# A polysketch attention with a rational feed-forward layer: buffers and linear parts by group instead of by chunk, with a new order

## The chip, the cores and the metric

The kernel runs on one core of a Trainium2 chip. The time is the device time of one execution in microseconds, the median of three runs. The profile is of one such execution. Engines: PE is TensorE (PEld its weight loads), DVE is VectorE, ACT is ScalarE, POOL is GpSimd, SP is SyncE. SP and ACT issue the plain loads and stores, POOL the accumulating transfers.

## What is computed

Attention with a feature map of 64 products for each head, for 4 batches, 4 heads, 1088 tokens and 32 dimensions, gives x of 4352 x 128. A feed-forward layer with 2048 hidden units follows; its activation is a rational function.

```python
def phi(x):
    a = np.einsum('rd,bhsd->bhsr', S1, x)          # r = 8
    b = np.einsum('rd,bhsd->bhsr', S2, x)
    return np.einsum('bhsi,bhsj->bhsij', a, b).reshape(*x.shape[:-1], r * r)
q_p, k_p = (phi(q), phi(k))
kv = np.einsum('bhsf,bhsd->bhfd', k_p, v)
z = np.sum(k_p, axis=2)
num = np.einsum('bhsf,bhfd->bhsd', q_p, kv)
den = np.einsum('bhsf,bhf->bhs', q_p, z)[..., None] + 1e-06
# x = num / den, heads put side by side
h = x @ w_in                                        # 128 -> 2048
h2 = h * h
P = a[0] + a[1] * h + a[2] * h2 + a[3] * h2 * h
Q = 1.0 + np.abs(b[0]) * np.abs(h) + np.abs(b[1]) * h2
return (P / (Q + 1e-06)) @ w_out
```

## The kernel before

The tokens are worked on in chunks of 512 (eight of them, 0 to 7) and a last one of 256 (8). For each chunk, h is computed transposed, 128 hidden units at a time: 16 slices of 128 x 512. The slices are taken in groups of 8 (g4 and g5 are chunk 1, ... g16 and g17 chunk 7); the first chunk has groups of 2, 2, 4 and 8 (g0 to g3), the last of 8, 4 and 4 narrower slices (g18 to g20). A full group is thus a tile of 128 x 4096 bf16, 1 MB.

The parameters are scaled so that Q is a constant times (1 + |y| + y^2) plus an offset, and 1/Q comes from a logarithm and an exponential on ACT. These are the steps of a group (names as in the text):

```python
h_mm       # PE:  h_ps = w_in^T x, two slices in a PSUM tile of 1024 (three tiles)
h_evac  e  # ACT (or DVE): hb = h_ps, to bf16
d_sq       # DVE: s = hb * hb                  tensor_tensor
d_ab       # DVE: u = |hb|                     tensor_scalar (bit mask)
us         # u += s                            accumulating DMA from POOL, or DVE
d_hi       # DVE: t = a3 * hb + a2             tensor_scalar
d_cu       # DVE: t = t * s                    tensor_tensor
d_lo       # DVE: hb = a1 * hb + a0            tensor_scalar
ts         # t += hb                           accumulating DMA from POOL, or DVE
ln, ex     # ACT: u = exp(-ln(... u + 1))
d_ov       # DVE: t = t * u                    tensor_tensor
project pj # PE:  out_ps += t^T w_out
```

Which sums and copies go to DVE is a table (ENGINE), and the order in which all steps are issued is a list of numbers (ORDER) found by a search. Each engine works through its own steps in that order. Buffers are taken when a step is issued and come free when the last step that gives them has been issued. In the kernel before, the buffers of the feed-forward part hold a whole chunk:

```python
BUFS = dict(xT=3, hb=2, s=1, u=2, t=2, ..., h_ps=3, out_ps=1, w_ps=1, ...)
FW = NF * CW                                        # 16 * 512 = 8192
SHAPES = dict(..., hb=([128, FW], BF), s=([128, FW], BF), u=([128, FW], BF), t=([128, FW], BF), ...)

WIDE = ["hi", "lo"]
def units(op):
    return whole if op in WIDE and 0 < n < len(chunks) else parts
...
def add(name, dst, src, f0, f1):
    if ENGINE.get(name) == "DVE":
        nc.vector.tensor_add(out=at(dst, f0, f1), in0=at(dst, f0, f1), in1=at(src, f0, f1))
    else:
        nc.gpsimd.dma_start(out=at(dst, f0, f1), in_=at(src, f0, f1), accum_op=AX.add, max_dma_last_dim=4096)
...
wide("sq", d_sq, "s", tt, ["e"])
wide("ab", d_ab, "u", ts, ["e"])
sum_of("us", "u", "s", ["sq", "ab"], [("s", n)])
wide("hi", d_hi, "t", tp, ["e", c_inv])
wide("cu", d_cu, None, tt, ["hi", "sq"], give=[("s", n)])
wide("lo", d_lo, None, tp, ["hi", "ab", "sq"])
sum_of("ts", "t", "hb", ["cu", "lo"], [("hb", n)])
```

So in chunks 1 to 7 the two linear parts, hi and lo, are one instruction each for the whole chunk (128 x 8192), and all else goes by group. Both kernels cut the first chunk's x into two halves of its tokens (SPLIT), so that the first h starts on the first half.

Before and beside this, for each batch the keys' features are made (transposes on PE, an evacuation, a projection, an evacuation `ea` of its first part, a product `pd` on DVE), kv is accumulated on PE and spread by four small copies (`s0`, `s1`, two each), and for each chunk of queries there are an evacuation `ev`, two expansions on PE, an evacuation `A`, a product on DVE, num and den on PE, a division of three DVE instructions, and a transpose with an evacuation `xe` that scales x by a number from the parameter b. An evacuation `eT` brings the output from PSUM. "Fills" are matmuls of zeros, two each, that only keep PE's clock up.

Of the kernel before, what the change touches and what calls it, by code (L numbers as in the profile page):

```python
# [12 lines left out]
FP = mybir.dt.float32  # L13
# [9 lines left out]

WIDE = ["hi", "lo"]
SPLIT = [0]
FILLS = 16

BUFS = dict(xT=3, hb=2, s=1, u=2, t=2, k_sb=2, v=1, q=2, L=1, h_ps=3, out_ps=1, w_ps=1,
# [3 lines left out]
    "ld.S0": "ACT", "ld.S1": "ACT", "ld.a": "ACT", "ld.b": "ACT", "k00.ea": "DVE", "k01.ea": "DVE", "k0.s0": "DVE",  # L32
    "q1.xe": "DVE", "k10.ea": "DVE", "k11.ea": "DVE", "k1.s0": "DVE", "k1.s1": "DVE", "q3.ev": "DVE", "k2.s1": "DVE",
    "k3.s0": "DVE", "q6.xe": "DVE", "q7.xe": "DVE", "g2.us": "DVE", "g4.e2": "DVE", "g4.us": "DVE", "g6.ts": "DVE",
    "g13.e0": "DVE", "g15.ts": "DVE", "g16.ts": "DVE", "g20.us": "DVE", "g19.ts": "DVE", "o8.eT": "DVE",
}

SKIP = ["f5", "f2", "f4", "f10", "f1"]

HOME = {  # L40
    "sT": "h_ps", "k01.T": "h_ps", "k01.ab": "h_ps", "kr.T": "h_ps", "kr.ab": "h_ps", "q0.T": "h_ps",
    "q0.xT.0": "h_ps", "q1.T": "h_ps", "q1.xT": "h_ps", "k10.T": "h_ps", "k11.T": "h_ps", "k11.ab": "h_ps",
    "kv.1": "h_ps", "q2.T": "h_ps", "q2.xT": "h_ps", "q3.T": "h_ps", "q3.xT": "h_ps", "k21.T": "h_ps",
    "kv.2": "h_ps", "q5.T": "h_ps", "k31.T": "h_ps", "q6.T": "h_ps", "q6.xT": "h_ps", "q7.xT": "h_ps",
    "fill.1": "h_ps", "fill.2": "h_ps", "fill.4": "h_ps", "fill.5": "h_ps", "fill.8": "h_ps", "fill.9": "h_ps",
    "fill.11": "h_ps", "fill.12": "h_ps", "fill.13": "h_ps", "fill.15": "h_ps",
# [3 lines left out]
    6, 28, 26, 30, 27, 1, 56, 0, 31, 32, 57, 4, 41, 42, 36, 7, 70, 71, 43, 37, 33, 58, 8, 20, 5, 38, 44, 46, 45, 60,  # L50
    59, 47, 21, 48, 81, 82, 49, 39, 40, 29, 51, 50, 52, 61, 53, 2, 72, 54, 3, 34, 55, 62, 74, 22, 10, 83, 64, 86, 87,
    23, 84, 85, 65, 66, 63, 67, 96, 97, 9, 73, 75, 68, 88, 89, 90, 218, 69, 219, 35, 220, 247, 11, 239, 235, 251, 16,
    221, 76, 222, 223, 255, 236, 224, 225, 77, 226, 12, 240, 248, 256, 252, 78, 24, 249, 227, 228, 243, 241, 229,
    237, 259, 25, 263, 231, 233, 245, 230, 244, 264, 232, 257, 234, 79, 253, 261, 98, 267, 271, 275, 80, 281, 100,
    242, 238, 260, 282, 268, 283, 265, 266, 250, 285, 287, 284, 286, 288, 254, 289, 290, 291, 292, 107, 246, 269,
    270, 273, 272, 258, 276, 91, 299, 262, 108, 99, 92, 93, 297, 101, 13, 95, 94, 301, 293, 102, 103, 104, 274, 118,
    295, 294, 105, 119, 296, 300, 298, 106, 309, 303, 109, 277, 278, 14, 133, 319, 321, 134, 111, 123, 320, 306, 304,
    279, 120, 18, 322, 124, 15, 110, 112, 305, 302, 310, 323, 324, 280, 325, 121, 307, 326, 122, 335, 327, 144, 328,
    145, 311, 113, 114, 115, 337, 313, 329, 125, 331, 333, 330, 135, 126, 127, 332, 334, 116, 137, 308, 160, 161,
    315, 117, 357, 339, 359, 312, 341, 338, 336, 361, 358, 128, 314, 360, 362, 347, 316, 129, 344, 342, 340, 130,  # L60
    131, 132, 343, 348, 136, 138, 363, 364, 162, 163, 365, 17, 139, 366, 140, 345, 141, 367, 164, 349, 19, 346, 368,
    369, 142, 143, 375, 373, 377, 370, 317, 371, 372, 318, 351, 395, 155, 146, 374, 376, 378, 379, 353, 396, 156,
    350, 397, 398, 399, 148, 400, 157, 170, 147, 171, 401, 382, 380, 383, 149, 385, 403, 405, 402, 150, 151, 158,
    381, 352, 384, 404, 406, 152, 159, 411, 413, 409, 386, 389, 407, 408, 172, 174, 153, 154, 410, 354, 355, 356,
    165, 387, 417, 414, 412, 433, 391, 434, 415, 166, 167, 168, 388, 435, 436, 420, 169, 437, 438, 418, 173, 175,
    416, 423, 390, 439, 440, 441, 181, 442, 419, 424, 443, 392, 449, 445, 176, 177, 421, 444, 182, 183, 422, 178,
    446, 451, 192, 179, 180, 427, 453, 425, 447, 448, 455, 393, 394, 473, 452, 450, 429, 185, 426, 471, 472, 454,
    474, 475, 476, 456, 184, 186, 477, 193, 458, 461, 187, 188, 459, 189, 479, 478, 480, 428, 194, 196, 462, 190,
    195, 191, 197, 457, 487, 489, 481, 482, 483, 460, 484, 485, 486, 430, 465, 488, 198, 199, 490, 463, 491, 431,
    432, 492, 464, 493, 511, 466, 496, 494, 509, 467, 510, 497, 513, 512, 514, 515, 516, 527, 495, 499, 200, 468,  # L70
    517, 518, 519, 521, 500, 520, 201, 523, 547, 522, 524, 549, 525, 529, 469, 470, 501, 498, 526, 503, 531, 502,
    528, 537, 211, 504, 532, 505, 205, 548, 534, 553, 550, 530, 506, 507, 215, 533, 551, 538, 558, 213, 564, 535,
    555, 508, 552, 208, 541, 539, 554, 560, 217, 557, 566, 536, 556, 563, 561, 559, 562, 570, 567, 573, 540, 543,
    210, 542, 214, 572, 569, 216, 580, 581, 565, 576, 577, 578, 544, 571, 575, 202, 545, 546, 568, 574, 209, 579,
    582, 583, 584, 585, 586, 587, 588, 207, 204, 589, 206, 212, 203,
# [40 lines left out]
def kernel(  # L116
# [27 lines left out]
    FW = NF * CW  # L144
# [14 lines left out]
    SHAPES = dict(xT=([128, CW], FP), hb=([128, FW], BF), s=([128, FW], BF), u=([128, FW], BF), t=([128, FW], BF),  # L159
# [408 lines left out]
    def add_chunk(n, W, sizes, g0, x_step, prev_o, store):  # L568
        rem = n == len(chunks)
        nsub = 1024 // W  # L570
        parts, f0 = [], 0
        for z in sizes:
            parts.append((f"g{g0 + len(parts)}", f0, f0 + z))
            f0 += z
        whole = [(f"w{n}", 0, NF)]

        def units(op):
            return whole if op in WIDE and 0 < n < len(chunks) else parts

        def at(buf, f0, f1):  # L580
            return T[buf, n][:, f0 * W:f1 * W]

        def h_mm(f0, cols=None):
            p = new("h_ps", n, f0) if cols in (None, 0) else T["h_ps", n, f0]
            c0, c1 = (0, W) if cols is None else (cols * W // 2, (cols + 1) * W // 2)
            for i in range(nsub):
                fi = f0 + i
                nc.tensor.matmul(p[:, i * W + c0:i * W + c1], lhsT=w_in_sb[:, fi * 128:(fi + 1) * 128],  # L588
                                 rhs=T["xT", n][:, c0:c1], start=True, stop=True)

        def h_evac(name, f0):
            if f0 == 0:
                new("hb", n)
            copy(name, at("hb", f0, f0 + nsub), T["h_ps", n, f0])

        def d_sq(f0, f1):
            nc.vector.tensor_mul(out=at("s", f0, f1), in0=at("hb", f0, f1), in1=at("hb", f0, f1))  # L597

        def d_ab(f0, f1):
            nc.vector.tensor_scalar(out=at("u", f0, f1).bitcast(mybir.dt.int16), in0=at("hb", f0, f1).bitcast(mybir.dt.int16),  # L600
                                    scalar1=0x7FFF, scalar2=None, op0=AX.bitwise_and)

        def d_hi(f0, f1):
            nc.vector.tensor_scalar(out=at("t", f0, f1), in0=at("hb", f0, f1), scalar1=a_sb[:, 3:4], scalar2=a_sb[:, 2:3],  # L604
                                    op0=AX.mult, op1=AX.add)

        def d_cu(f0, f1):
            nc.vector.tensor_mul(out=at("t", f0, f1), in0=at("t", f0, f1), in1=at("s", f0, f1))  # L608

        def d_lo(f0, f1):  # L610
            nc.vector.tensor_scalar(out=at("hb", f0, f1), in0=at("hb", f0, f1), scalar1=a_sb[:, 1:2], scalar2=a_sb[:, 0:1],  # L611
                                    op0=AX.mult, op1=AX.add)

        def add(name, dst, src, f0, f1):
            if ENGINE.get(name) == "DVE":
                nc.vector.tensor_add(out=at(dst, f0, f1), in0=at(dst, f0, f1), in1=at(src, f0, f1))  # L616
            else:
                nc.gpsimd.dma_start(out=at(dst, f0, f1), in_=at(src, f0, f1), accum_op=AX.add, max_dma_last_dim=4096)  # L618

        def ln(f0, f1):  # L620
            nc.scalar.activation(out=new("L", n, f0)[:, :(f1 - f0) * W], in_=at("u", f0, f1), func=ACT.Ln, bias=one_ap, scale=lsc)  # L621

        def ex(f0, f1):
            nc.scalar.activation(out=at("u", f0, f1), in_=T["L", n, f0][:, :(f1 - f0) * W], func=ACT.Exp, scale=-1.0)  # L624

        def d_ov(f0, f1):
            nc.vector.tensor_mul(out=at("t", f0, f1), in0=at("t", f0, f1), in1=at("u", f0, f1))  # L627
# [157 lines left out]
```

## Time and profile before

| | |
|---|---|
| time | 250.15 us, median of 3 runs (250.06 to 250.33) |
| span of the profiled execution | 248.3 us, mean granted TensorE clock 0.978 |
| accumulating transfers u<-s of 1 MB | 14, median 9.5 us from issue to landing |
| accumulating transfers t<-hb of 1 MB | 12, median 8.7 us |
| DVE, first polynomial instruction of g0 | at 25.77 us |
| DVE, last instruction (output evacuation) | at 244.60 us |
| DVE waiting for t<-hb; ACT waiting for u<-s | 1.0 us; 2.9 us in all |

How the profile is read. A line of the busy list gives each engine's busy time and its share of the span. A row of digits gives the busy share in 40 equal slices, in tenths. A queue line gives packets, MB, and the time that its packets took as a share of the 16 DMA engines. A line of the table by windows begins with the window and its length; then come the busy us of PE, PEld, DVE, ACT and POOL with the instruction counts, the granted clock, the DMA share and GB/s. A line of the chain gives the start, the duration and the work. A group line has the source line, engine, operation, tiles and shapes, count, then busy us and mean ns of one, and at the end the idle time ahead of it and its cause.

### The profile page before, as it was taken

The page shows a single profiled execution, that of the slowest core. Times are in us where ns is not written, and L with a number is a line of the kernel's source. Part 1 is how long each engine was busy: PE and PEld are TensorE (multiplying, and loading weights), DVE is VectorE, ACT ScalarE, POOL GpSimd, SP SyncE. Part 2 cuts the span into 40 slices and gives each one's busy share as a digit, 9 for nine tenths or more (in the row PEclk, how much of TensorE's full clock was granted, in tenths as well). Part 3 has the DMA queues.
Part 4 walks back from the last instruction along what each step waited for, and adds up shares of the span by engine and source line. Part 5 has one row for each costly group of instructions (what it writes and reads, how often), then busy time and mean ns, then how long its engine had stood idle before and what let it go on. Part 6 is the DMA issues. An engine that isn't in the chain of part 4 may idle for free.

```text
span 248.3 us, 4269 instructions
## 1 busy us (share of the span) xinstructions
PE 223.7 (90%) x1785; PEld 130.3 (53%) x1785; DVE 229.1 (92%) x204; ACT 215.5 (87%) x161; POOL 49.3 (20%) x59
## 2 busy tenths in 40 slices
PE   8979999999999999999999999998999966780773
PEld 4656444475745547546456735553465525650652
DVE  1658999999999899999999999999999999999993
ACT  3532579989999999999999999998999799999990
POOL 4000514210222110103231050202133021103120
PEclk9999999999999999999999999999999999997679
DMA  6796394979289999769999969999999989396872
GB/s 206 203 298 208 53 128 86 185 139 221 82 161 203 190 170 164 187 117 197 162 172 191 209 108 183 188 209 179 174 160 198 202 145 182 86 201 117 163 144 65
DMA packets 22627, 41.18 MB, mean 166 GB/s; under 512 B 5200, under 2 KB 13520, under 8 KB 22608
## 3 DMA queue, kind: packets, MB, share of 16 engines
q0 software_dynamic: 10432, 30.94, 71.7%
q1 hardware_dynamic: 11712, 9.90, 12.5%
q8 instruction: 14, 0.23, 0.4%
q10 hardware_dynamic: 464, 0.08, 0.2%
q14 instruction: 5, 0.04, 0.1%
HBM read 8.79 MB, written 2.23 MB: 44 GB/s over the span
## 4 chain that ended last, share of the span: by engine, by line
PE 60%; DVE 20%; DMA 9%; issue 5%; ACT 4%; POOLq 0%; DVEq 0%; ACTq 0%
PE h_ps L588 34%; PE out_ps L634 7%; PE h_ps L483 6%; DVE t L627 5%; DMA u<-s 5%; PE h_ps L503 3%; DVE t L608 3%; DVE t L604 2%; PE h_ps L405 2%; DVE hb L611 2%; DVE s L597 2%; DMA t<-hb 2%; DMA b_sb<-in_moe_b_dram 2%; DVE u L600 2%; ACT hb L187 2%
## 5 line engine op out<-in xcount | busy, mean ns | idle before, releaser
L588 PE MATMUL h_ps<-xT,w_in_sb 128*128 128x512 f32 (+1 forms) x292 | 125.2, 572 | 2.6 <-ACT xT L537 2.1
L588 PEld LDWEIGHTS h_ps<-xT,w_in_sb 128*128 128x128 f32 x292 | 52.7, 190 | 55.8 <-issue 43.5
L187 ACT CAST hb<-h_ps 128x1024 bf16<-128x1024 f32 x66 | 65.9, 1019 | 9.9 <-PE h_ps L588 9.4
L621 ACT ACTIVATE L<-u,one_ap,lsc 128x4096 f32<-128x4096 bf16 (+2 forms) x21 | 66.4, 3163 | 3.0 <-DMA u<-s 2.9
L624 ACT ACTIVATE u<-L 128x4096 bf16<-128x4096 f32 (+2 forms) x21 | 62.5, 2976 | 0.2
L634 PE MATMUL out_ps<-w_out,t 128*128 128x128 bf16 x544 | 36.9, 230 | 13.6 <-DVE t L627 13.6
L618 POOL DMA_DIRECT2D u<-s x18 | 25.9, 1436 | 116.0 <-DVE s L597 61.5
L634 PEld LDWEIGHTS <-t 128*128 128x128 bf16 x544 | 34.1, 104 | 21.9 <-DVE t L627 18.6
L627 DVE TENSOR_TENSOR t<-t,u 128x4096 bf16<-128x4096 bf16 (+2 forms) x21 | 39.3, 1880 | 1.4 <-DMA t<-hb 1.0
L597 DVE TENSOR_TENSOR s<-hb 128x4096 bf16<-128x4096 bf16 (+2 forms) x21 | 39.5, 1879 | 0.6 <-ACT hb L187 0.5
L608 DVE TENSOR_TENSOR t<-t,s 128x4096 bf16<-128x4096 bf16 (+2 forms) x21 | 39.4, 1878 | 0.1
L618 POOL DMA_DIRECT2D t<-hb x17 | 20.0, 1260 | 73.5 <-DVE t L608 52.6
L611 DVE TENSOR_SCALAR hb<-hb,a_sb 128x8192 bf16<-128x8192 bf16 (+3 forms) x14 | 23.2, 1657 | 0.1
L604 DVE TENSOR_SCALAR t<-hb,a_sb 128x8192 bf16<-128x8192 bf16 (+3 forms) x14 | 22.0, 1569 | 0.3 <-ACT hb L187 0.3
L600 DVE TENSOR_SCALAR u<-hb 128x4096 int16<-128x4096 int16 (+2 forms) x21 | 21.3, 1017 | 0.0
L483 PE MATMUL h_ps<-qT,Srep 64*128 64x512 f32 (+1 forms) x72 | 19.5, 617 | 0.4 <-DVE x L517 0.3
L503 PEld LDWEIGHTS h_ps<-kv,q_pT 128*64 128x64 f32 (+1 forms) x288 | 8.9, 134 | 7.2 <-issue 5.6
L490 DVE TENSOR_TENSOR q_pT<-A_sb,h_ps 128x1024 f32<-128x1024 f32 (+1 forms) x9 | 10.4, 1157 | 0.8 <-PE h_ps L483 0.7
L503 PE MATMUL h_ps<-kv,q_pT 128*64 128x66 f32 (+1 forms) x288 | 10.4, 225 | 0.6 <-DVE q_pT L490 0.6
L187 ACT COPY A_sb<-h_ps 128x1024 f32<-128x1024 f32 (+1 forms) x9 | 8.8, 973 | 0.6 <-PE h_ps L483 0.4
L483 PEld LDWEIGHTS h_ps<-qT,Srep 64*128 64x128 f32 x72 | 5.4, 184 | 5.9 <-ACT hb L187 2.6
L616 DVE TENSOR_TENSOR t<-t,hb 128x4096 bf16<-128x4096 bf16 (+1 forms) x4 | 7.5, 1886 | 0.0
(89 smaller groups left out, 139.6 us busy)
## 6 DMA issues: line engine op xcount, KB each, us to landing
u<-s POOLq DMA_DIRECT2D x14, 1024.0 KB, 9.5
t<-hb POOLq DMA_DIRECT2D x12, 1024.0 KB, 8.7
q<-in_q_dram SPq DMA_DIRECT2D x8, 256.0 KB, 4.8
k_sb<-in_k_dram SPq DMA_DIRECT2D x4, 512.0 KB, 5.7
v<-in_v_dram SPq DMA_DIRECT2D x4, 512.0 KB, 6.8
out_dram<-oT SPq DMA_DIRECT2D x8, 256.0 KB, 6.2
w_in_sb<-in_moe_w_in_dram SPq DMA_DIRECT2D x2, 512.0 KB, 5.6
t<-hb POOLq DMA_DIRECT2D x2, 512.0 KB, 5.6
```

What stands on the lines that cost most here:

```text
L187: nc.scalar.copy(out=out, in_=in_)
L483: nc.tensor.matmul(pair(i)[:, g, :W], lhsT=Srep[i][rows].rearrange("p g f -> p (g f)"), rhs=T["qT", n][rows, :W], start=True, stop=True)
L588: nc.tensor.matmul(p[:, i * W + c0:i * W + c1], lhsT=w_in_sb[:, fi * 128:(fi + 1) * 128], rhs=T["xT", n][:, c0:c1], start=True, stop=True)
L597: nc.vector.tensor_mul(out=at("s", f0, f1), in0=at("hb", f0, f1), in1=at("hb", f0, f1))
L604: nc.vector.tensor_scalar(out=at("t", f0, f1), in0=at("hb", f0, f1), scalar1=a_sb[:, 3:4], scalar2=a_sb[:, 2:3], op0=AX.mult, op1=AX.add)
L608: nc.vector.tensor_mul(out=at("t", f0, f1), in0=at("t", f0, f1), in1=at("s", f0, f1))
L611: nc.vector.tensor_scalar(out=at("hb", f0, f1), in0=at("hb", f0, f1), scalar1=a_sb[:, 1:2], scalar2=a_sb[:, 0:1], op0=AX.mult, op1=AX.add)
L618: nc.gpsimd.dma_start(out=at(dst, f0, f1), in_=at(src, f0, f1), accum_op=AX.add, max_dma_last_dim=4096)
L621: nc.scalar.activation(out=new("L", n, f0)[:, :(f1 - f0) * W], in_=at("u", f0, f1), func=ACT.Ln, bias=one_ap, scale=lsc)
L624: nc.scalar.activation(out=at("u", f0, f1), in_=T["L", n, f0][:, :(f1 - f0) * W], func=ACT.Exp, scale=-1.0)
L627: nc.vector.tensor_mul(out=at("t", f0, f1), in0=at("t", f0, f1), in1=at("u", f0, f1))
L634: nc.tensor.matmul(T["out_ps", n][:, j * 128:(j + 1) * 128], lhsT=T["t", n][:, fi * W + j * 128:fi * W + (j + 1) * 128], rhs=W_out[:, fi, ...
```

## The change

The feed-forward steps are written by group again. Every one of them, hi and lo too, works on its group's 128 x 4096; the four kinds of buffers are half as wide and twice as many, so that they take the same room, and a group takes and gives back its own. The engines of some sums and copies, the places of small PSUM tiles, the fills, the loads' order and the order of all steps come from another search, which allowed for ACT and DVE instructions to overlap. What it is for: each buffer comes free with its group instead of with its chunk, which gives the order more freedom; the price is twice as many instructions for hi and lo.

```diff
-WIDE = ["hi", "lo"]
-BUFS = dict(xT=3, hb=2, s=1, u=2, t=2, k_sb=2, v=1, q=2, L=1, h_ps=3, out_ps=1, w_ps=1,
+BUFS = dict(xT=3, hb=4, s=2, u=4, t=4, k_sb=2, v=1, q=2, L=1, h_ps=3, out_ps=1, w_ps=1,
 ENGINE = {
     "ld.S0": "ACT", "ld.S1": "ACT", "ld.a": "ACT", "ld.b": "ACT", "k00.ea": "DVE", "k01.ea": "DVE",
-    "k0.s0": "DVE", "q1.xe": "DVE", "k10.ea": "DVE", "k11.ea": "DVE", "k1.s0": "DVE", "k1.s1": "DVE",
-    "q3.ev": "DVE", "k2.s1": "DVE", "k3.s0": "DVE", "q6.xe": "DVE", "q7.xe": "DVE",
-    "g2.us": "DVE", "g4.e2": "DVE", "g4.us": "DVE", "g6.ts": "DVE", "g13.e0": "DVE", "g15.ts": "DVE",
-    "g16.ts": "DVE", "g20.us": "DVE", "g19.ts": "DVE", "o8.eT": "DVE",
+    "kr.ea": "DVE", "k0.s0": "DVE", "q1.ev": "DVE", "q1.xe": "DVE", "k10.ea": "DVE", "q3.xe": "DVE",
+    "k20.ea": "DVE", "k30.ea": "DVE", "k31.ev": "DVE", "q6.xe": "DVE", "q8.ev": "DVE", "q8.A": "DVE",
+    "q8.xe": "DVE", "g1.us": "DVE", "g1.ts": "DVE", "g6.e6": "DVE", "g17.us": "DVE", "o7.eT": "DVE",
+    "g18.us": "DVE", "g20.us": "DVE", "g20.ts": "DVE", "o8.eT": "DVE",
 }
-SKIP = ["f5", "f2", "f4", "f10", "f1"]             # fills left out
+SKIP = ["f2", "f10", "f8"]
 ...                                                # HOME and ORDER: other lists
-    FW = NF * CW
+    GW = GF * CW                                   # 8 * 512 = 4096
-    SHAPES = dict(..., hb=([128, FW], BF), s=([128, FW], BF), u=([128, FW], BF), t=([128, FW], BF), ...)
+    SHAPES = dict(..., hb=([128, GW], BF), s=([128, GW], BF), u=([128, GW], BF), t=([128, GW], BF), ...)
 ...
-        wide("hi", d_hi, "t", tp, ["e", c_inv])
-        wide("cu", d_cu, None, tt, ["hi", "sq"], give=[("s", n)])
-        wide("lo", d_lo, None, tp, ["hi", "ab", "sq"])
-        sum_of("ts", "t", "hb", ["cu", "lo"], [("hb", n)])
+        d2 = plan.add(nm + ".ab", "DVE", ts, d_abs, after=[he], take=[("u", g)])
+        d1 = plan.add(nm + ".sq", "DVE", tt, d_sq, after=[he], take=[("s", g)])
+        us = add_sum(nm + ".us", "u", "s", [d1, d2], [("s", g)])
+        hi = plan.add(nm + ".hi", "DVE", tp, d_high, after=[he, c_inv], take=[("t", g)])
+        p = plan.add(nm + ".cu", "DVE", tt, d_cube, after=[hi, d1], give=[("s", g)])
+        w = plan.add(nm + ".lo", "DVE", tp, d_low, after=[hi, d2, d1])
+        tsum = add_sum(nm + ".ts", "t", "hb", [p, w], [("hb", g)])
 ...
```

In the new order the first loads are q of chunk 1, k of batch 0, q of chunk 0 and the second half of w_in, then k's rest, k of batch 1 and v of batch 0; the parameter b is issued from ACT two copies earlier. Of the fills, one pair comes at g11 and two at g12 and g13, the others near the end; before, all were near the end.

## The prediction

> **What bounds the kernel now.** I read the page first: the busy line, the DMA row of the forty slices, the DMA queues.
>
> ```profile
> PE 223.7 (90%) x1785; PEld 130.3 (53%) x1785; DVE 229.1 (92%) x204; ACT 215.5 (87%) x161; POOL 49.3 (20%) x59
> ...
> DMA  6796394979289999769999969999999989396872
> ...
> q0 software_dynamic: 10432, 30.94, 71.7%
> q1 hardware_dynamic: 11712, 9.90, 12.5%
> ```
>
> Three engines are within 14 us of one another, and the 16 DMA engines carry 71.7 + 12.5 = 84% of the span. No single engine is "the" bound, so the second view is the table by windows (busy us of each engine in 25 us, then the granted clock, the DMA share and GB/s):
>
> ```profile
> 50.00:75.00 25.00, 25.00 (x244) 15.04 (x243) 24.74 (x21) 23.74 (x18) 4.71 (x3) 1.00 0.75 152
> 75.00:100.00 25.00, 25.00 (x243) 15.00 (x242) 23.90 (x18) 23.24 (x21) 3.57 (x3) 1.00 0.99 177
> 100.00:125.00 25.00, 25.00 (x156) 12.70 (x155) 24.86 (x17) 24.69 (x19) 5.91 (x4) 1.00 0.84 168
> 125.00:150.00 25.00, 25.00 (x225) 14.42 (x224) 24.89 (x18) 24.55 (x19) 6.28 (x4) 1.00 0.93 171
> 150.00:175.00 25.00, 24.01 (x182) 12.90 (x180) 24.71 (x20) 24.16 (x17) 4.76 (x4) 1.00 1.02 188
> 175.00:200.00 25.00, 24.26 (x176) 13.59 (x174) 24.90 (x18) 23.23 (x16) 5.81 (x4) 1.00 0.98 180
> 200.00:225.00 25.00, 16.80 (x115) 11.44 (x113) 24.49 (x14) 24.93 (x15) 3.47 (x4) 1.00 0.77 148
> ```
>
> From 50 to 200 us PE, DVE and ACT all have under 8% of idle time, and from 75 us on the DMA share is 0.84 to 1.02. The reader should see that everything is full at once: work taken from one engine is only worth something if it isn't put on another that has no room. The third view, the chain that ended last, changes owner accordingly: TensorE from 19 to 155 us, DVE and ACT with some accumulating DMAs after that.
>
> ```profile
> 145.72 3.63 PE h_ps L588 x8
> ...
> 183.45 11.74 DMA u<-s
> ...
> 235.78 5.14 DMA t<-hb
> ```
>
> The transfer issued at 183.45 took 11.74 us because another megabyte, issued at 179.98 us by the GpSimd timeline, was ahead of it: a queue, not a latency. The same view limited to 125 to 200 us, for the queues, gives the price of one:
>
> ```profile
> q0 software_dynamic: 3279, 12.60, 94.3%
> q1 hardware_dynamic: 432, 0.79, 3.1%
> ```
>
> 12.60 MB are 12 transfers of 1 MB, and 94.3% of 75 us is 70.7 us: 5.9 us of all 16 engines for each.
>
> **The Trainium skill.** "VectorE: DVE Perf Modes", section "The perf-mode tier table", puts bf16 tensor_scalar at four elements per cycle and tensor_tensor at two, and the section on the TRN2 errata says that each instruction pays a fixed part that a larger tile pays once. The trace agrees:
>
> ```profile
> L597 DVE TENSOR_TENSOR s<-hb 128x4096 bf16<-128x4096 bf16 x15 | 34.3, 2287 | 0.6 <-ACT hb L187 0.5
> L604 DVE TENSOR_SCALAR t<-hb,a_sb 128x8192 bf16<-128x8192 bf16 x7 | 16.9, 2407 | 0.0
> L604 DVE TENSOR_SCALAR t<-hb,a_sb 128x4096 bf16<-128x4096 bf16 x1 | 1.3, 1344 | 0.0
> ```
>
> One of 8192 takes 2407 ns and two of 4096 take 2688. "DMA: Bandwidth & Descriptors", section "SWDGE vs HWDGE vs iDMA", says that an accumulating DMA can only be issued from GpSimd, and "Issuing engines are not separate DMA queues" that all issuers share the same 16 engines: the sums, the loads and the stores compete, as the shares above add up.
>
> **The change, part by part.** I laid each engine's instructions of the two orders end to end, each with its pitch (start to start where the timeline has them back to back): 2.20 us for a tensor_tensor of 4096, 1.13 for the absolute value, 1.26 and 2.32 for a linear part of 4096 and 8192, 1.13 for an evacuation of h or a k feature product on DVE, 0.4 for a kv spread.
>
> 1. Linear parts: seven chunks had two instructions of 8192 and get four of 4096. 14 x (2 x 1.26 - 2.32) = +2.8 us of DVE.
> 2. Sums. Of the full-size sums, group 4's u+s and those of t+hb in groups 6, 15 and 16 were on DVE; they go to DMAs. Group 17's u+s comes to DVE. Net -3 x 2.2 = -6.6 us of DVE. The smaller sums on DVE go from one of 2048 and two of 1024 to one of 2048 and four of 1024: 2 x 0.6 = +1.2. Together -5.4.
> 3. Copies: one h evacuation fewer on DVE (-1.1), four kv spreads fewer (-1.6), but q and k evacuations, x evacuations, the last A and an output evacuation more (+2.6). About -0.1.
> 4. Sum for DVE: +2.8 - 5.4 - 0.1 = -2.7; summing instruction by instruction gives 226.9 before and 224.6 after, -2.3 us. ACT is 209.7 against 209.8, PE 213.2 against 214.0: two more fill pairs at 0.43 each, three pairs of them now in the middle, where PE has no idle time.
> 5. DMA: the sums were 29 MB in all (26 of 1 MB and 3 MB of smaller ones) and become 31.5. Three more of 1 MB in the full stretch at 5.9 us are +17.7 us; over the kernel, 2.5 x 5.9 = +14.8 us.
> 6. Buffers: two of 8192 (one for s) become four of 4096 (two for s), in the same bytes. A group gives its half back without waiting for its chunk's other half. It allows other orders; it takes no time by itself.
> 7. Start. Now the parameter b arrives at 17.26 us and DVE has idled 2.3 us for it. The new order issues b before the last copies of the keys' features, and DVE turns to g0 with 14.5 us of work behind it against 14.1. The load of v0 goes behind half of w_in (0.5 MB, about 1.5 us at the 336 GB/s of the window from 4 to 8 us). Following the path b, first division, two transposes, first h, I get g0's first polynomial at 25.1 us instead of 25.77: -0.6.
>
> If nothing else changed, the end would move by -2.3 - 0.6 = -2.9 us. Against it stands part 5. From 50 to 225 us the seven windows above average a DMA share of 0.90, 157 us of 175; 17.7 more make 174.7 of 175. The densest long stretch there is, 125 to 200 us, had 94.3 + 3.1 = 97%. At that density the same work takes 180 us, 5 us longer. The new order does leave a 1 MB sum 6 to 17 us of other DVE work before its reader at most places. Laying the transfers behind one another at 6.5 us each (loads included; 6.1 where only stores are left), I find those of t in groups 10, 15, 16 and 17 landing within 1 us of their reader, and s of group 17 freed within 1 us of its writer. Delays of DVE elsewhere loosen that a little, but a queue at its limit doesn't hold every appointment: I put +4 to +5 us for it, and +0.4 for fills in the middle. -2.9 + 4.4 + 0.4 = +1.9 us: 252.0 us.
>
> **The rivals.** (a) DVE decides and the DMA queue just keeps up: 250.15 - 2.9 = 247.2. For it: the new order spaces consumers widely, and the old one ran windows at 0.98 to 1.02 with DVE idle under 0.3 us in 25. Against: it has room for one late transfer, not for a queue. (b) The DMA queue becomes the bound from about 75 us to the end, its gaps at the ramp can't be refilled, and each late sum holds ACT (which waits for u) and DVE (which waits for t): 14.8 us minus the 5 to 8 that the old gaps can take, +7 to +10: 257 to 260. For it: the 11.74 us transfer on the chain, ACT's four waits for u<-s (2.9 us). Against: 0.75 at 50 to 75 and 0.77 at 200 to 225 can be filled. (c) TensorE goes on being the chain to 155 us and the middle doesn't move at all; then only start and tail count. The tail has less on DVE after group 17's last product (about 9 us against 10), two small sums instead of DMAs for group 20: -1 to +0.5 us, 249.5 to 250.5.
>
> **Range and chances.** (a), (b), (c) and the mixed case at 0.15, 0.15, 0.25 and 0.45 put the middle near 252. The range 248.2 to 256.5 leaves out a pure (a) or (b). Over 2% faster would be below 245.1, which needs more than all of DVE's gain: 0.03. Over 2% slower, above 255.2, needs a good half of (b): 0.17. Within 2%: 0.80.
>
> **What would show it.** Right: DVE busy about 2 us lower or equal; q0 at 76 to 79% and about 33.5 MB; DMA shares of 0.95 or more in all windows from 50 to 200; median landing of 1 MB sums up from 9.5 and 8.7 us to 10 to 12; waits of the product with u for t<-hb, now 1.0 us, and of Ln for u<-s, now 2.9 us, growing to some 5 us together. Step 7 is right if the first polynomial instruction starts at 24.5 to 25.5. Wrong: if landings stay where they are and both waits stay below 3 us, (a) or (c) holds and the time is at or below 250; if DVE idles by 8 us and more in front of sums, (b). A PE that idles in the middle without any DMA wait would point to a cause that I haven't counted, the depth of three h buffers in the new order.

## The result and the profile after

| | before | after |
|---|---|---|
| time, median of 4 runs each | 250.24 us (250.06 to 250.76) | 247.26 us (246.79 to 248.07) |
| ratio, with its 95% interval | | 0.9881 [0.9851, 0.9911] |
| span of the profiled execution | 248.3 us | 245.6 us |

The changed kernel is 3.0 us faster. The prediction was 252.0 us with a range of 248.2 to 256.5, so the time lies below the range, and the sign was wrong.

The page of the changed kernel: the busy list, the DMA row of the forty slices, the DMA queues, and the landing times of the 1 MB sums (size, then the median us from issue to landing).

```profile
PE 223.5 (91%) x1789; PEld 129.3 (53%) x1789; DVE 226.4 (92%) x215; ACT 215.5 (88%) x163; POOL 48.8 (20%) x60
...
DMA  6984599999999799997999989999699999996870
...
q0 software_dynamic: 10960, 33.56, 77.1%
q1 hardware_dynamic: 11712, 9.90, 13.2%
...
t<-hb POOLq DMA_DIRECT2D x15, 1024.0 KB, 9.6
u<-s POOLq DMA_DIRECT2D x14, 1024.0 KB, 9.2
```

DVE has 2.7 us less to do, ACT the same, and the queue of the sums carries 2.62 MB more. But a sum of 1 MB lands in 9.2 and 9.6 us, where the kernel before had 9.5 and 8.7. The queue is fuller and hardly later.

The table by windows of the changed kernel, for the seven windows shown of before:

```profile
50.00:75.00 25.00, 25.00 (x222) 13.36 (x219) 23.78 (x20) 23.82 (x20) 5.19 (x5) 1.00 1.00 179
75.00:100.00 25.00, 25.00 (x233) 15.07 (x228) 24.90 (x19) 24.38 (x17) 5.20 (x4) 1.00 0.99 193
100.00:125.00 25.00, 25.00 (x201) 14.45 (x201) 24.31 (x21) 24.46 (x22) 5.11 (x5) 1.00 0.94 183
125.00:150.00 25.00, 24.89 (x186) 13.68 (x186) 25.00 (x17) 24.77 (x18) 3.92 (x4) 1.00 0.98 189
150.00:175.00 25.00, 24.76 (x235) 14.26 (x235) 23.73 (x22) 22.30 (x17) 4.41 (x4) 1.00 0.92 170
175.00:200.00 25.00, 24.76 (x147) 13.48 (x136) 24.72 (x19) 24.65 (x18) 5.74 (x4) 1.00 1.03 189
200.00:225.00 25.00, 15.72 (x101) 11.35 (x101) 25.00 (x20) 24.93 (x12) 6.52 (x5) 0.81 0.93 172
```

The DMA share, the last number but one, rose where there was room: 0.75 to 1.00 in the window from 50 us, 0.84 to 0.94 from 100 us, 0.77 to 0.93 from 200 us. In us these three are 6.25, 2.5 and 4.0. The window from 25 to 50 us (0.76 before, 0.88 after) took another 3.0. So the new transfers stand in the old gaps.

Nor did ACT or DVE wait much for them. All their waits for a sum, from the list of waits of the changed kernel (us in total, times, longest):

```profile
ACT L L622 <- DMA u<-s: 1.7, 3, 0.9
```

Before, these were 2.9 us of ACT and 1.0 us of DVE. DVE's wait for t<-hb is gone from the list.

The chain that ended last, in the changed kernel:

```profile
118.37 3.63 PE h_ps L580 x8
...
144.73 11.76 DMA u<-s
156.57 3.81 ACT L L622
...
182.53 5.22 PE h_ps L580 x12
...
195.07 3.70 ACT L L622
...
233.52 1.92 ACT u L626
```

TensorE owns it to 123 us and again from 165 to 188 us. One sum of 11.76 us is on it, as in the kernel before. After 188 us ACT has it almost to the end.

Where the 3 us are in the trace: two views by windows, the kernel before and then the one after, for 25 to 200 us and for what is left after 200 us.

```profile
25.00:200.00 175.00, 173.27 (x1315) 95.18 (x1314) 172.49 (x137) 163.86 (x122) 39.42 (x29) 1.00 0.90 164
200.00:250.00 50.00, 28.55 (x221) 20.85 (x219) 43.23 (x35) 42.11 (x24) 7.19 (x8) 0.87 0.70 135
```

```profile
25.00:200.00 175.00, 174.38 (x1313) 96.50 (x1312) 171.34 (x141) 166.07 (x129) 37.82 (x30) 1.00 0.96 179
200.00:250.00 50.00, 26.49 (x208) 18.08 (x207) 40.92 (x38) 39.93 (x21) 8.26 (x7) 0.82 0.72 137
```

At 200 us all three engines are ahead by about the same: PE has 2.1 us less left, DVE 2.3, ACT 2.2. DVE is ahead although it worked less until then, because it has less to do; ACT and PE are ahead because they idled less. Three engines that advance together are coupled, and the trace alone doesn't say which pulls. That is what the runs are for.

A part of the gain comes later still. The last Ln on ACT starts 1.73 us earlier than before (237.83 against 239.56), but the last evacuation 2.70 us earlier. The ends of the two chains, before and after:

```profile
241.01 1.24 DVE t L627
...
242.30 1.64 PE out_ps L634 x24
...
244.60 0.42 DVE oT L189
```

```profile
240.49 0.70 DVE t L629
...
241.24 0.63 PE out_ps L637 x8
...
241.90 0.42 DVE oT L189
```

Before, a product of 2048 columns has waited for its sum (the transfer issued at 235.78, shown in the prediction), and 32 projection matmuls still follow it. After, both sums of g20 are on DVE, and only the 8 matmuls of the last product of 1024 columns are left. That is about 1.0 of the 2.7 us of span. No run takes this part by itself.

### The profile page after: what moved, and what is told of

Its sections match the earlier page's. It is cut to its first block, busy times and chain, and to the rows that moved or that the text cites. A ratio compares the mean times of both kernels' runs of the same rounds, so it can differ in the third digit from the quotient of the medians.

```text
span 245.6 us, 4296 instructions
## 1 busy us (share of the span) xinstructions
PE 223.5 (91%) x1789; PEld 129.3 (53%) x1789; DVE 226.4 (92%) x215; ACT 215.5 (88%) x163; POOL 48.8 (20%) x60
## 2 busy tenths in 40 slices
DMA packets 23155, 43.80 MB, mean 178 GB/s; under 512 B 5216, under 2 KB 13536, under 8 KB 23136
## 3 DMA queue, kind: packets, MB, share of 16 engines
q0 software_dynamic: 10960, 33.56, 77.1%
## 4 chain that ended last, share of the span: by engine, by line
PE 56%; ACT 20%; DVE 9%; DMA 7%; issue 6%; SPq 0%; DVEq 0%; ACTq 0%
PE h_ps L580 33%; ACT u L626 9%; ACT L L622 8%; PE out_ps L637 6%; PE h_ps L483 5%; DMA u<-s 5%; PE h_ps L503 4%; ACT hb L187 3%; DVE t L629 2%; PE w_ps L405 2%; DVE s L590 2%; DMA q<-in_q_dram 2%; PE h_ps L405 1%; DVE t L611 1%; DVE u L593 1%
## 5 line engine op out<-in xcount | busy, mean ns | idle before, releaser
L187 ACT CAST hb<-h_ps 128x1024 bf16<-128x1024 f32 x67 | 66.6, 1021 | 7.1 <-PE h_ps L580 6.6
L637 PE MATMUL out_ps<-w_out,t 128*128 128x128 bf16 x544 | 36.1, 226 | 14.6 <-DVE t L629 14.6
L637 PEld LDWEIGHTS <-t 128*128 128x128 bf16 x544 | 32.9, 102 | 22.2 <-DVE t L629 19.4
L602 POOL DMA_DIRECT2D u<-s x17 | 22.0, 1296 | 95.8 <-DVE u L593 47.8
L602 POOL DMA_DIRECT2D t<-hb x19 | 23.3, 1242 | 87.9 <-ACT hb L187 33.3
L611 DVE TENSOR_SCALAR t<-hb,a_sb 128x4096 bf16<-128x4096 bf16 (+2 forms) x21 | 25.0, 1193 | 0.0
L618 DVE TENSOR_SCALAR hb<-hb,a_sb 128x4096 bf16<-128x4096 bf16 (+2 forms) x21 | 23.7, 1137 | 0.0
L187 ACT COPY A_sb<-h_ps 128x1024 f32<-128x1024 f32 x8 | 8.1, 1014 | 0.9 <-PE h_ps L483 0.8
L517 DVE TENSOR_TENSOR x<-h_ps,den 128x512 f32<-128x512 f32 (+1 forms) x10 | 6.1, 611 | 0.3
```

The costliest lines, as they stand in the source:

```text
L187: nc.scalar.copy(out=out, in_=in_)
L602: nc.gpsimd.dma_start(out=d, in_=s, accum_op=AX.add, max_dma_last_dim=4096)
L611: nc.vector.tensor_scalar(out=new("t", g)[:, :gw], in0=T["hb", g][:, :gw], scalar1=a_sb[:, 3:4], scalar2=a_sb[:, 2:3], op0=AX.mult, op1=AX ...
L637: nc.tensor.matmul(T["out_ps", n][:, j * 128:(j + 1) * 128], lhsT=T["t", g][:, c:c + 128], rhs=W_out[:, fis[i], :], start=fis[i] == 0 and ...
```

## The experiments

The theory at this point was that TensorE sets the pace of the middle and the queue costs nothing. The rivals were: the sums' queue sets it; DVE sets it and its 2.3 us are the gain; ACT sets the tail. "Before" in the tables is the time of the kernel before, measured together with the run.

**1. Is anything gained by taking work away from one resource of the changed kernel?** Four runs leave work out between about 50 and 150 us. What they leave out is named in each diff, so these are times of a part of the computation.

```diff
 after_less_dma: sums t += hb of g6, g8, g10, g12 left out (4 MB, 23.6 us of the queue)
+            if name in ("g6.ts", "g8.ts", "g10.ts", "g12.ts"):
+                return
 after_less_dve: second linear part of the same groups left out (5.0 us of DVE)
+            if g in (6, 8, 10, 12):
+                return                                    # in d_low
 after_less_act: Exp at half its width in g6, g8, g10 (5.2 us of ACT)
+            if g in (6, 8, 10):
+                lw = lw // 2
 after_less_pe: projection of two slices of eight in g6, g8, g10, g12 (5.4 us of PE)
-            for i in range(len(fis)):
+            for i in (0, 7) if g in (6, 8, 10, 12) else range(len(fis)):
```

> The changed kernel with the sums t+hb of groups 6, 8, 10 and 12 left out (those outputs lack their low part): four transfers of 1 MB less, 4 x 5.9 = 23.6 us of the DMA engines, nothing else changed. If the DMA queue sets the time (the 4.4 us that I had put in for it), -4 us or more: 243 or below. If the queue only keeps up and DVE or another engine decides: within 1 us of 247.3. If all are coupled: -1 to -2.

> The changed kernel with the linear part of hb left out in groups 6, 8, 10 and 12 (four DVE instructions of 1.26 us, 5.0 us in all; the sums read the unscaled hb). If DVE decides, -4 to -5 us: 242.5 to 243.5. If the queue decides, within 1 us of 247.3. If PE, ACT and DVE are coupled, -1 to -2 us.

> The changed kernel with the exponential done on half the width in groups 6, 8 and 10 (three times 1.73 us of ACT, 5.2 us; half of each of those groups keeps its denominator undivided). If ACT is the chain (the tail of it is, by the profile after), -3 to -5 us; if DVE decides, within 1 us of 247.3; coupled, -1 to -2.

> The changed kernel with six of the eight slices of the projection left out in groups 6, 8, 10 and 12 (4 x 1.35 = 5.4 us of PE, the output lacks those slices). The chain that ended last goes along PE to 123 us, so if PE decides the middle, -3 to -5 us; if DVE or ACT decides, within 1 us of 247.3.

| run | time, us | before, us | against 247.26 |
|---|---|---|---|
| after_less_dma | 247.09 (246.84 to 247.27) | 249.92 | -0.2 |
| after_less_dve | 246.87 (246.80 to 247.03) | 249.92 | -0.4 |
| after_less_act | 247.68 (246.97 to 249.46) | 249.92 | +0.4 |
| after_less_pe | 245.12 (245.01 to 246.16) | 249.92 | -2.1 |

Only TensorE's cut stands out of the spread of the changed kernel (246.79 to 248.07): 2.1 us, 0.4 for each us left out. The sizes named in the edits are counted by instruction; by the busy lists DVE lost 4.3 us, ACT 5.1 and PE 4.4. The queue theory falls here, for the middle of the kernel. This is the DMA row of the page with four sums left out:

```profile
DMA  6984599899999775993199919980699999996870
```

It has holes (the 5, 3, 1, 1 and 0 in the middle) that the row of the changed kernel does not have, and the time is the same. A queue at 0.96 of its capacity over 175 us cost nothing that these runs can show.

**2. Each engine's neighbour, and the tail.** When TensorE has less to do, who is next, and does ACT or DVE set the last 60 us?

```diff
 after_less_dve_and_pe: both cuts above
 after_less_pe_and_act: both cuts above
 after_less_act_late: Exp at half its width in the tail (5.2 us of ACT)
+            if g in (14, 15, 16):
+                lw = lw // 2
 after_less_dve_late: second linear part left out in the tail (3.8 us of DVE)
+            if g in (15, 16, 17):
+                return                                    # in d_low
```

> The changed kernel with both cuts: the linear part of hb and six of eight projection slices left out in groups 6, 8, 10 and 12 (5.0 us of DVE, 5.4 us of TensorE). Alone they brought 0.4 and 2.1 us. If DVE is the bound right behind TensorE: -4 us or more, 243 and below. If ACT or the DMA queue is behind it: 244.5 to 245.5.

> The changed kernel with the cut of TensorE's work in groups 6, 8, 10 and 12 (-5.4 us) and Exp at half its width in groups 6, 8 and 10 (-5.2 us of ACT; leaves out parts of the computation). The cut of TensorE alone gave 245.1, that of ACT alone 247.7. If ACT stands right behind TensorE in the middle, both together give 242.5 to 244. If DVE or the sums stand behind it, 244.7 to 245.3.

> The changed kernel with Exp at half its width in groups 14, 15 and 16 (-5.2 us of ACT, between about 165 and 210 us; leaves out part of the computation). If ACT sets the tail after 185 us, as the chain has it, 242.5 to 245. If DVE and the sums set it, 246.5 to 247.3.

> The changed kernel without the second linear part of groups 15, 16 and 17, three VectorE instructions of 4096 between about 200 and 222 us, 3.8 us (leaves out part of the computation). If VectorE's late work sets the end, 243.3 to 244.8. If the sums or ACT stand right behind it, 245.5 to 246.5; if VectorE counts as little as in the middle, 246.7 to 247.3.

| run | time, us | before, us |
|---|---|---|
| after_less_dve_and_pe | 244.77 (244.57 to 246.03) | 249.84 |
| after_less_pe_and_act | 245.21 (244.74 to 246.83) | 250.00 |
| after_less_act_late | 247.25 (246.90 to 247.85) | 250.00 |
| after_less_dve_late | 246.95 (246.74 to 247.62) | 250.10 |

A second cut adds nothing to TensorE's 2.1 us that stands out of the spread (-0.4 for DVE, +0.1 for ACT). In the tail, neither ACT nor DVE can be relieved alone, although the chain named ACT and DVE had no gap from 176 to 239 us. I had expected 243.3 to 244.8 for the last run if DVE's late work set the end; it doesn't, alone.

The traces of the two late cuts show what stands next. With less DVE, the chain stays with ACT from 188 us on. With less ACT, it goes over to a sum: t<-hb, issued at 203.21 us behind another issued at 200.78, takes 13.53 us, ACT waits 2.1 us for the hb buffer that it gives back, and DVE's product follows at 217.86 us. So in the tail ACT stands level with DVE and with a buffer held by a late sum. The queue, which costs nothing in the middle, does hold the end once ACT is relieved. ACT and DVE were not cut there together.

**3. The same in the kernel before.**

```diff
 before_less_dve: second linear part of chunks 3 and 4 left out (4.6 us of DVE)
+            if n in (3, 4):
+                return                                    # in d_lo
 before_less_pe: projections of the first halves of chunks 2 to 5 cut to two slices (5.4 us of PE)
-            for fi in range(f0, f1):
+            for fi in (f0, f1 - 1) if n in (2, 3, 4, 5) and f0 == 0 else range(f0, f1):
```

> The kernel before with the wide linear part of hb left out in chunks 3 and 4 (two DVE instructions of 2.32 us, 4.6 us in all; the sums read the unscaled hb). If DVE's work is what the change saves on, this should bring -2.5 to -4.6 us: 245.5 to 247.5. If TensorE sets the middle, as the four leave-outs in the changed kernel say there, within 1 us of 250.1.

> The kernel before, with the projections of the first half of chunks 2 to 5 cut from eight slices to two (leaves out part of the sum of the output; about -5.4 us of TensorE between 50 and 150 us). If TensorE's stream sets the middle of the kernel before as it does in the one after (there 5.4 us less gave 2.1), 247.5 to 248.5. If DVE or the DMA sums set it in the old order, 249.5 to 250.3.

Measured: 250.44 us against 249.84 without DVE's 4.6 us (ratio 1.0016 [1.0002, 1.0031]), and 249.96 against 250.00 without PE's 5.4 us (0.9991 [0.9968, 1.0013]). Neither alone brings anything. The chain by engine shows why; first before_less_dve, then before_less_pe:

```profile
PE 63%; DVE 19%; DMA 7%; issue 5%; ACT 4%; POOLq 0%; DVEq 0%; ACTq 0%
```

```profile
DVE 47%; PE 25%; DMA 12%; issue 10%; ACT 4%; POOL 0%; SPq 0%; DVEq 0%; ACTq 0%; POOLq 0%
```

In the unaltered kernel before, PE has 60% of the chain and DVE 20%. Take DVE's work away and the chain stays with PE; take PE's away and it goes over to DVE. I read this as two engines that stand level, each of which holds the end alone. Both cuts together were not tried, and the shares are of one execution each: in before_b_early (experiment 5), where only the start moved, PE has 40% and DVE 39%. So a saving of DVE of 2.3 us could not be counted in full, as the prediction did; in the old order, less DVE work alone would not have brought the time of the change.

**4. Putting the parts of the change back, one at a time.** Here work is added to an order or moved within it, instead of taken away.

```diff
 before_parts_by_group: both linear parts by group in the old order, buffers as they were
-WIDE = ["hi", "lo"]
+WIDE = []
 before_sums_moved: the old order, with the new engines of five full-size sums
-    "g4.us": "DVE", "g6.ts": "DVE", "g15.ts": "DVE", "g16.ts": "DVE",
+    "g17.us": "DVE",
 after_sums_back: the new order, with the old engines of the same five sums
-    "g17.us": "DVE",
+    "g4.us": "DVE", "g6.ts": "DVE", "g15.ts": "DVE", "g16.ts": "DVE",
```

> The kernel before with hi and lo as one instruction for each group, one behind the other at the place of the wide one; buffers and order stay. DVE gets 14 x 0.2 = 2.8 us. If DVE decides: 252.5 to 253. If another engine decides: 250 to 251.

> The kernel before with the change's choice for the full-size sums only: u+s of group 4 and t+hb of groups 6, 15, 16 from DVE to DMAs, u+s of group 17 from a DMA to DVE; the order and all else stay. DVE loses 6.6 us, the DMA engines get 17.7 us. If DVE's work decides and the queue keeps up: 250.2 less 3 to 6, so 244 to 247. If the queue is full: 251 to 256. If it depends on the order whether a landing is met: near 250 with DVE waiting for t<-hb by 3 us or more.

> The changed kernel with the full-size sums where the kernel before has them: u+s of group 4 and t+hb of groups 6, 15, 16 on DVE, u+s of group 17 a DMA; order and all else stay. DVE gets 6.6 us, the DMA engines lose 17.7 us. If DVE decides: 251 to 254. If the queue decides: 243 to 247. If the order takes the difference up: within 1 us of 247.3.

| | sums as before | sums as after |
|---|---|---|
| old order, parts by chunk | 250.07 | 264.37 (1.0573 [1.0519, 1.0627]) |
| old order, parts by group | 252.02 (1.0071 [1.0040, 1.0102]) | not tried |
| new order, parts by group | 252.04 (1.0078 [1.0059, 1.0097]) | 247.26 (0.9881 [0.9851, 0.9911]) |

The ratios are to the kernel before. With parts by group and the old sums, the old order takes 252.02 us and the new one 252.04: the new order, with all that came with it (buffers, small sums, copies, loads, fills), brings nothing without the five sums. They are worth -4.8 us in the new order and cost +14.3 in the old one. So the 3 us are +1.95 for the parts by group and -4.8 for three sums more on DMAs, and what the new order and its buffers are good for is that they make the second possible. The order was found for the new sums, and an order searched for the old ones might take less than 252; that wasn't tried.

Order and buffers are not told apart. The old order has its parts and its buffers by chunk where the sums cost 14.3 us, and neither the cell that wasn't tried nor the new order with the old buffers was run.

What a sum costs that misses its appointment is seen in the waits of before_sums_moved, and in the DVE timeline of the worst of them:

```profile
DVE t L627 <- DMA t<-hb: 8.9, 4, 6.0
ACT L L621 <- DMA u<-s: 8.6, 5, 5.7
...
PE w_ps L471 <- DMA q<-in_q_dram: 3.8, 1, 3.8
ACT hb L187 <- DMA t<-hb: 3.8, 2, 2.4
```

```profile
225.72 2.29 DVE L627 TENSOR_TENSOR t<-t,u 128x4096 bf16<-128x4096 bf16 x1 [6.02 <-DMA t<-hb]
```

For ACT and DVE that is 21.3 us of waiting where the kernel before had 3.9. 3.8 of them are ACT's, for an hb buffer that here comes back only with its chunk; the changed kernel has no such wait. TensorE's 3.8 us are for a load of q: it was issued at 54.99 us, just behind the moved sum of g4 (54.90), and took 13.41 us by the chain. The two sums that GpSimd issued ahead of this product, from its timeline:

```profile
209.87 1.21 POOL L618 DMA_DIRECT2D u<-s  x1 [4.03 <-issue]
210.59 1.70 POOL L618 DMA_DIRECT2D t<-hb  x1
```

They come 0.7 us apart, and the second, the one that the product reads, took 15.04 us by the chain. The DMA row of this run, whose queues carry almost the same bytes as the changed kernel's (44.33 MB against 43.80):

```profile
DMA  6685597899899939999999699999999799039971
```

It is no fuller on the whole. The 0 and the 3 are 223 to 236 us: the queue is crowded until the late sum lands, DVE stands still for it, and then the queue is empty until DVE has made the inputs of the next sum. And a 1 MB sum lands as fast as in the changed kernel, in the median:

```profile
t<-hb POOLq DMA_DIRECT2D x15, 1024.0 KB, 9.2
u<-s POOLq DMA_DIRECT2D x14, 1024.0 KB, 9.5
```

So the lateness comes from where sums, loads and readers stand in the order, and from when buffers come free, and not from the rate of the queue.

The other half, after_sums_back, shows what DVE's work costs when it is added. Its page, busy list and chain:

```profile
PE 223.1 (89%) x1784; PEld 130.0 (52%) x1789; DVE 232.5 (93%) x218; ACT 215.3 (86%) x163; POOL 44.9 (18%) x57
...
PE 48%; DVE 36%; issue 8%; DMA 5%; ACT 1%; SPq 0%; POOL 0%; DVEq 0%; POOLq 0%; ACTq 0%
```

6.1 us more of DVE make 4.8 us of time, 0.8 us for each, and DVE's part of the chain rises from 9% to 36%. The parts by group added 2.6 us of DVE (231.7 against 229.1) for 1.95 us, again 0.75 for each. Yet 5.0 us less brought 0.4. This fits an engine that stands level with another: what is added counts, what is taken away doesn't. It is argued and not shown: the added work and the cuts lie at different places, and neither order was searched for the added work.

**5. The start.** In the new order the parameter b is loaded earlier, and g0's first polynomial starts earlier.

```diff
 before_b_early: the old order, load of b moved
     ... kr.ev
+    ld.b
     ...
-    ld.b
 after_b_late: the new order, load of b moved behind k0.s1, the second spread of kv of batch 0
```

> The kernel before with the load of the parameter b issued from ACT ahead of the loads of v's rest, three copies earlier; nothing else. DVE should no longer wait 2.3 us for b, and the first division should begin at about 16.5 us instead of 18.1. If the gain at the start carries to the end: 248.6 to 249.4. If the middle takes it back: 250.0 to 250.3.

> The changed kernel with the load of the parameter b issued from ACT two copies later, behind the spread of kv: it lands near 20 us instead of 13, and DVE waits for it ahead of its own kv spread, so that num, den, x and the first h start some 4 us later. Nothing else changes. If the start sets how far TensorE is ahead and the middle has no slack to win it back: +3 to +4.5 us, 250 to 252. If the middle absorbs it: +1 or less.

before_b_early took 248.84 us (0.9943 [0.9926, 0.9960]), after_b_late 252.67 (1.0121 [1.0096, 1.0146]). With b early, g0's first polynomial starts at 23.91 instead of 25.77 us, 1.86 earlier. How far does that travel? The last Ln instructions on ACT's timeline, first of the kernel before, then of before_b_early:

```profile
224.84 3.83 ACT L621 ACTIVATE L<-u,one_ap,lsc 128x4096 f32<-128x4096 bf16 x1
...
239.56 1.24 ACT L621 ACTIVATE L<-u,one_ap,lsc 128x1024 f32<-128x1024 bf16 x1
```

```profile
223.00 3.83 ACT L621 ACTIVATE L<-u,one_ap,lsc 128x4096 f32<-128x4096 bf16 x1
...
237.71 1.24 ACT L621 ACTIVATE L<-u,one_ap,lsc 128x1024 f32<-128x1024 bf16 x1
```

The whole of it: 1.84 us at 225 us and 1.85 at 240. In these two orders, fixed and with next to no slack, the shift of the start is passed on undiminished for 200 us. By the medians 1.2 of the 1.85 us are left at the end. The profiled execution, the slowest of its eleven, shows where its own rest went: DVE's product that waits for the t<-hb sum of g18 starts 1.84 us earlier than before (239.17 against 241.01), but the 32 projection matmuls after it take 3.50 us instead of 2.27, at a granted clock of 0.53 instead of 1.00, and the last evacuation is only 0.62 us earlier.

In after_b_late DVE waits 6.03 us for b, and the last Ln comes 6.44 us later (244.27 against 237.83), 5.4 us by the medians, more than the 3 to 4.5 expected. The spread of kv is 4.81 us late (20.17 against 15.36) and the first h 6.94 (27.09 against 20.15): the difference arises in the half-speed matmuls of the last section.

**6. A rebuild of the gain in the old order.** b early, and one DVE instruction of 2.3 us less near the end, where the trace has DVE 2.3 us ahead.

```diff
 before_b_early_less_dve_late: before_b_early, second linear part of chunk 7 left out
+            if n == 7:
+                return                                    # in d_lo
```

> The kernel before with b loaded early (which alone gave 248.8) and without the second linear part of chunk 7, one VectorE instruction of 8192 at about 219 us, 2.3 us (leaves out part of the computation). If VectorE's late work sets the end, the two causes add up to the changed kernel's time: 246.3 to 247.3. If the end is set by TensorE, ACT or the sums, 248.4 to 249.0.

Measured: 247.82 us (0.9909 [0.9874, 0.9944]), between the two expectations. DVE's late 2.3 us are worth about 1.0 on top of b's 1.2. So late in the kernel, where PE is no longer level, DVE's work counts by some 0.4 in the old order; in the new order 3.8 us brought 0.3 (experiment 2). Neither theory of the tail holds as it was stated.

**7. Fills.** Three pairs of filling matmuls stand in the middle of the new order, where TensorE has no gap to fill.

```diff
 after_no_middle_fills
-SKIP = ["f2", "f10", "f8"]
+SKIP = ["f2", "f10", "f8", "f6", "f5", "f1"]
 after_fewer_fills
+SKIP = ["f2", "f10", "f8", "f6", "f5", "f1", "f3", "f0"]
```

> The changed kernel without the three fill pairs in the middle (f6, f5, f1: 3 x 0.43 = 1.3 us of TensorE). Leaving out 5.4 us of projections brought 2.1 us, 0.4 of each us. If TensorE's work counts wherever it lies: -0.5 us, 246.6 to 246.9. If TensorE only waits at those places for something else: within 0.2 us of the changed kernel, or slower should the clock fall.

> The changed kernel without the pairs of filling matmuls f6, f5, f1 and also f3 and f0 (about -2.2 us of TensorE). Without the first three it took 246.6. If every us of TensorE's work still counts by 0.4, 246.2 to 246.5. If the first fills hold the clock up, a lower granted clock after them and 247 or more.

246.63 us (246.51 to 248.10, six runs) and 246.69 (246.50 to 246.92, four runs), against 247.26 (246.79 to 248.07). Both are the best medians among kernels that do the whole computation, 0.6 us below the changed kernel, but the runs overlap, and the five pairs are no better than the three. I take it as a likely gain, not a shown one.

## Why the prediction was wrong, by its own steps

1. *Linear parts, +2.8 us of DVE.* Right: +2.6 measured (before_parts_by_group), and 1.95 us of time.
2. *Sums, -6.6 us of DVE for the full-size ones.* Right in size: 6.1 (after_sums_back). In time they are worth 4.8 us, in the new order with its buffers only.
3. *Copies, -0.1*, and 4. *-2.3 for DVE together*: the busy list has -2.7. ACT is equal, as said. PE is 0.2 lower where 0.8 more was said.
5. *The queue, "+4 to +5 us": this is the step that failed.* Its quantities were right: 77.1% of q0 (76 to 79 said), 33.56 MB (33.5), shares of 0.92 to 1.03 from 50 to 200 us (0.95 or more said). What didn't follow was lateness. Landings of 10 to 12 us were said and 9.2 and 9.6 measured; waits of 5 us, and 1.7 measured. The step took the share of the densest stretch, 97%, for a limit and turned the bytes into time by it. But a queue's share says how much it carries, not whether a reader waits. That depends on how far each sum stands from its reader and on what it holds up meanwhile: the old order with the new sums waited 21.3 us, the new order with the same five sums 1.7, at shares of 0.93 and 0.96 over 25 to 200 us. I had laid the transfers out and found the closest within 1 us of their readers, and then trusted the average more than the layout. Leaving four sums out (0.2 us) shows that the term is near zero in the middle. The sign that the prediction had named for this, both waits below 3 us, is what the trace has.
6. *Buffers, no time by themselves.* Not tested apart. The 3.8 us that ACT waited for hb buffers in before_sums_moved show that a buffer given back late can cost time.
7. *The start, -0.6.* The first polynomial starts at 25.07 us, 25.1 was said. The DVE timeline of the changed kernel:

```profile
24.34 0.74 DVE L355 TENSOR_SCALAR a_sb<-a_sb,inv 128x3 f32<-128x3 f32 x3
25.07 0.43 DVE L593 TENSOR_SCALAR u<-hb 128x1024 int16<-128x1024 int16 x1
```

Experiment 5 shows that such a shift is passed on. Fills in the middle, +0.4, fit the 0.6 of experiment 7, which is likely and not shown.

Without step 5 the sum is -2.9 + 0.4, 247.6 us, and 247.26 was measured. That is in part luck, since DVE's 2.3 us were counted in full and the 1.0 us of the last few us stands in no step. "DVE decides", rival (a), had the number (247.2) for a reason that only half holds. DVE's added work costs 0.75 to 0.8 us for each us, and for that reason its saving in the sums pays; but less DVE work than the changed kernel has brought nothing that stands out of the spread. Rival (c), that TensorE goes on being the chain to 155 us, had the right engine (after_less_pe is the only single cut of the changed kernel that stands out of the spread) and the wrong number, since it held the middle to be unmovable. Rival (b) fell.

The Trainium skill, "Perfetto Trace Analysis", section "Identifying the Most-Contended Engine", says to take the engine with the highest occupancy as the most contended and to optimize it first, and that TensorE's matmul busy time is no good measure. In the changed kernel DVE has the highest occupancy, 92%, with PE at 91% by the measure it warns of and 53% by the weight loads, which it names instead, beside the share of the peak rate. Here the measurement differs: 5.0 us less of DVE gave 0.4 us, 5.4 us less of PE gave 2.1.

What stays open: how much the end of the changed kernel would gain if ACT and DVE were both relieved after 188 us, how much of the sums' gain is due to the order and how much to the buffers by group, and how much of the 3 us is due to the start and how much to the sums, since the new order with the old sums has the earlier start too and takes 252.04.

## What to carry to other kernels

Where several engines are level, test a cost by adding work as well as by removing it: removal shows little where another engine stands right behind, while adding shows what a saving elsewhere has to pay for. A DMA queue near its full share isn't by itself a bound; look at the distance of each transfer from its reader in the order at hand, and at what its buffers hold up: the same move of work was worth -4.8 us in one order and +14.3 in another. Engine assignments and order are one choice, so a diff of assignments can't be priced without the order it comes with.

## What the runs showed of the hardware

One thing wasn't expected. In after_b_late TensorE idles for 4.58 us up to 20.78 us, and after it the same matmuls take twice as long; its PE timeline:

```profile
15.06 1.13 PE L483 MATMUL h_ps<-qT,Srep 64*128 64x512 f32 x4
20.78 1.15 PE L503 MATMUL h_ps<-kv,q_pT 128*64 128x66 f32 x16 [4.58 <-DVE kv L454]
...
24.58 2.08 PE L483 MATMUL h_ps<-qT,Srep 64*128 64x512 f32 x4
26.59 0.67 PE L367 MATMUL w_ps<-ident,k_sb 128*128 128x128 f32 x4
```

Four matmuls of 64x512 take 1.13 us before the gap and 2.08 after it. The four transposes at 26.59 us have the 0.66 us of the changed kernel again, some 6 us after the gap's end. The windows of the same run give the granted clock as 0.53 from 20 to 27 us:

```profile
20.00:27.00 7.00, 6.12 (x58) 4.01 (x59) 3.81 (x13) 0.47 (x1) 0.00 (x0) 0.53 0.05 15
```

The Trainium skill, "TensorE: Matmul & The Clock Gate", part 1 on the clock gate, says that the clock falls to half after at least one idle stretch of about 3.4 us and comes back after at least one as long of sustained work. The 0.53 and the doubled durations agree with the first; the way back took some 5.8 us here, with TensorE busy for 6.12 of the 7 us. So this late load cost its wait and then some us of half-speed matmuls. The tail shows the same: behind gaps of 7.01 us before and 8.10 after, 32 projection matmuls take 3.60 us, against 1.96 at 211 and 207 us. In the full middle there is no such gap: from 25 to 200 us the granted clock is 1.00 with the fills and without them (after_no_middle_fills), and there the fills are only work.
